# Plain second token product, an earlier hash and a plainly stored last row in an attention and mixer kernel

## The chip, the cores and the metric

The kernel runs on one core of a Trainium2 chip. The metric is the device time of one execution in microseconds (us); lower is better. Time before: 816.98 us, the median of three runs (815.75 to 818.22). The profiled execution spans 815.1 us from its first instruction to its last.

## The reference

Hash attention, then one mixer block. There are 4 batches, 8 heads, 768 tokens and 64 values per head; all is float32.

```python
def _attn_ref(q, k, v, proj):
    q_bits = (np.einsum('bhsd,dk->bhsk', q, proj) > 0)      # 6 bits, likewise k_bits
    ...                                                     # bucket = sum of bits * powers of two
    mask = q_bucket[:, :, :, None] == k_bucket[:, :, None, :]
    scores = scale * np.matmul(q, k.transpose(0, 1, 3, 2))
    scores = np.where(mask, scores, -1000000000.0)
    ...                                                     # softmax over the keys
    return np.matmul(attn, v)

def _moe_ref(x, w_tok1, w_tok2, w_ch1, w_ch2):              # x: (4, 768, 512)
    xt = x.transpose(0, 2, 1)
    h = np.maximum(xt @ w_tok1, 0.0) @ w_tok2               # token mixing: 768 -> 256 -> 768
    u = x + h.transpose(0, 2, 1)
    h2 = np.maximum(u @ w_ch1, 0.0) @ w_ch2                 # channel mixing: 512 -> 1536 -> 512
    return u + h2
```

## The kernel before

It has three stages: attention over 16 pairs of heads (a batch `b` and two heads `hp` each), the token products of the four batches, and the channel products. `XT` holds x and then u for the whole problem in on-chip memory, with channels on the partitions. Each engine takes its instructions in order, and waits where their inputs or buffers aren't ready.

**Attention.** Every pair has two halves of 384 queries. The hash bits of the next pair are made by a matmul, a comparison on VectorE, a scaling on ScalarE, and eight small DMAs that spread the rows. The first pair's bits are made in another way (`first_hashes`).

```python
        def hashes(n):
            g = pool.tile([P, HALF], BF16, name="g", tag="g", bufs=2)
            ps = psum.tile([P, 2, 512], F32, name="hp", tag="sc", bufs=3)[:, 0]
            for j in range(4):
                ...                                          # matmul hp <- projection, qk
            nc.vector.tensor_scalar(g, ps[:, :HALF], 0.0, 0.5, op0=ALU.is_gt, op1=ALU.subtract)
            nc.scalar.mul(g, g, bitscale)
            for j in range(4):
                for i in range(2):
                    ...
                    nc.sync.dma_start(out=bitrows[n % 2][...], in_=g[at : at + NB + 1])

        for n in range(len(pairs)):
            ...
            for now in halves:
                now.scores()        # sc <- qk, sc <- bits on TensorE, e <- sc on ScalarE
                now.add()           # sums of e on VectorE
                if now.half == 0:
                    now.add_last()
            if before:
                before.sums()
            if n + 1 < len(pairs):
                hashes(n + 1)
            halves[1].add_last()
            ...
            halves[0].weigh()       # acc <- e, v on TensorE
```

**Token stage.** `mix1` makes the first product (6 matmuls of 512 columns for each of two blocks) with its relu. `mix2` is the second product and the residual: plain for batch 0, and for batches 1 to 3 by Strassen's scheme in Winograd's form, with seven products of a half-sized matmul in place of eight, sums of the left blocks (`left_sums`) and of the weights (`weight_sums`) on VectorE. The result is assembled in one of three staging places, and a DMA that adds puts it into `XT`. Between these, `job()` takes one piece from a list: the sums of the first channel weights, then the conversion of w_ch2 from doubles (`slot`).

```python
        def mix2(b, m):
            ...
            ps = [bank("t2")[:, :HALF] for _ in range(4)]        # 8 PSUM banks in turn
            to = places[(2 * b + m + 1) % 3]...
            p1, u, p7, p57 = ...                                 # four quarters of that place

            def store():
                nc.gpsimd.dma_start(
                    out=XT[:, m::2, S * b : S * b + S], in_=to..., accum_op=ALU.add,
                )

            if not b:
                ...                                              # 8 plain matmuls, 4 copies on ScalarE
                return store()
            product(0, a00, b00)
            nc.scalar.copy(p1, ps[0])                            # line 695
            product(1, a01, b10)
            product(2, s1, sums[:, 0])
            nc.scalar.copy(p57, ps[2])                           # line 698
            product(3, new[:, 1], b01)
            nc.scalar.copy(p7, ps[3])                            # line 700
            product(0, new[:, 0], sums[:, 1], False)
            nc.scalar.copy(u, ps[0])                             # line 702
            product(2, new[:, 2], b11, False)
            product(3, a11, sums[:, 2], False)
            nc.vector.tensor_tensor(p1, ps[1], p1, op=ALU.add)   # line 705
            nc.gpsimd.tensor_tensor(p57, p7, p57, op=ALU.add)    # line 706
            nc.vector.tensor_tensor(p57, p57, u, op=ALU.add)     # line 707
            nc.vector.tensor_tensor(p7, ps[3], u, op=ALU.add)    # line 708
            nc.vector.tensor_tensor(u, ps[2], u, op=ALU.add)     # line 709
            store()                                              # line 673

        for b in range(B):
            mix1(b)
            if b:
                left_sums(b)
                mix2(b - 1, 0)
                job()
                mix2(b - 1, 1)
            if b == 1:
                weight_sums()
        mix2(B - 1, 0)
        inputs(0, T, 0)                                          # sums for the channel stage
        mix2(B - 1, 1)
```

**Channel stage.** All is Strassen there, in two groups of token columns. Line 774 is the matmul of a helper that the whole stage uses, 780 a copy out of PSUM. A group's outputs come from seven products, p1 to p7. Most output blocks are stored by a GpSimd DMA that adds to a residual (u) stored there earlier by a plain DMA. In the last product of the last group (p4, with `final`), VectorE completes four quarters, and each goes out by a plain DMA of its own.

```python
            if final:                                             # end of product(), p4 of the last group
                nc.vector.tensor_tensor(qs[:, 3], qs[:, 3], u, op=ALU.add)
                ...
                for i, a in [(1, ps[2]), (2, ps[3])]:
                    nc.vector.tensor_tensor(qs[:, i], a, qs[:, i], op=ALU.add)          # line 1193
                    (nc.scalar if i == 2 else nc.sync).dma_start(out=final(...), in_=qs[:, i])
                return
            ...
                product(s, 5, "p2", q2, [*end, add(q7, q7, XT[:, KC:, sl[0]])])
                product(s, 6, "p4", q7, [
                    add(q2, q2, q1), store(q2, 0, 0),             # adding store of the first row, 512 KB
                ], lambda i, n: out[...])
```

Of the kernel before, what the change touches and what calls it, by code (L numbers as in the profile page):

```python
# [48 lines left out]
def kernel(  # L49
# [14 lines left out]
    P = 128  # L64
# [75 lines left out]
    class Conversion:  # L140


        def __init__(self, pool, parts, bufs, apart=False):
            self.pool, self.bufs, self.apart = pool, bufs, apart
            self.todo = [
                (w, dst, rows, j, n)
                for w, dst, rows, blocks in parts
                for j in range(*blocks, rows)
                for n in range(0, dst.shape[2], NW // rows)
            ]  # L150
            self.fetched, self.begun, self.ready = [], None, None
            for _ in range(bufs - 1):
                self.fetch()
# [17 lines left out]
        def begin(self):  # L171
            if not self.fetched:
                return
            raw, to, rows = self.fetched.pop(0)
            hi = raw[:, :, 1]
            tmp = self.pool.tile([P, 2, NW], F32, name="tmp", tag="cvt", bufs=1)
            big = tmp[:, 0].bitcast(U32)

            nc.vector.tensor_scalar(  # L179
                big, hi, 3, 0x3FFFFFFF, op0=ALU.logical_shift_left, op1=ALU.bitwise_and,  # L180
            )
            nc.vector.scalar_tensor_tensor(
                big, hi, 0xC0000000, big, op0=ALU.bitwise_and, op1=ALU.bitwise_or,
            )
            self.begun = raw, tmp, to, rows
# [16 lines left out]
        def end(self):  # L202
# [5 lines left out]
            hi = size  # L208
            if self.apart:
                size = self.pool.tile([P, NW], F32, name="size", tag="size", bufs=1)  # L210
            nc.scalar.activation(size, hi, ACT.Square)
# [11 lines left out]
        def slot(self):  # L223

            self.end()
            self.fetch()
            self.begin()
            self.join()

# [6 lines left out]
    def bounce(stage, n):  # L236

        b, hp = pairs[n]
        stage = stage.rearrange("p (a k i) -> p a k i", k=2, i=32)
# [26 lines left out]
    def attention(pool, psum, W1, W2, x0):  # L266
# [202 lines left out]
        for n in range(len(pairs)):  # L469
# [3 lines left out]
            for now in halves:  # L473
                now.scores()
                now.add()
                if now.half == 0:
                    now.add_last()
            if before:
                before.sums()
            if n + 1 < len(pairs):  # L480
                hashes(n + 1)
# [21 lines left out]
            if n and n % 2 == 0:  # L503
                bounce(pool.tile([P, 2 * S], F32, name="stage", tag="stage", bufs=1), n - 2)
# [93 lines left out]
    def tokens(pool, psum, W1, W2, x0, weights, jobs, T, places):  # L598

# [7 lines left out]
        if not turned:  # L607
            fetch(1, x1)
            jobs = jobs(weights(pool))
            bounce(places[2], len(pairs) - 2)  # L610
        NQ = DM // 2
        sums = pool.tile([P, 3, HALF], F32, name="W2sums", tag="W2sums", bufs=1)
        b00, b01, b10, b11 = (W2[:, k, HALF * n : HALF * n + HALF] for k in range(2) for n in range(2))

        def weight_sums():
            nc.vector.tensor_tensor(sums[:, 0], b01, b00, op=ALU.subtract)
            nc.vector.tensor_tensor(sums[:, 1], b11, sums[:, 0], op=ALU.subtract)
            nc.vector.tensor_tensor(b01, b11, b01, op=ALU.subtract)
            nc.vector.tensor_tensor(sums[:, 2], b10, sums[:, 1], op=ALU.subtract)
# [11 lines left out]
        def mix1(b):  # L631
# [16 lines left out]
            if b % 2:  # L648
                new = pool.tile([P, 3, NQ], F32, name="r1s", tag="r1s", bufs=1)
            else:  # L650
                new = T[0].rearrange("p k t -> p (k t)")[:, : 3 * NQ].rearrange("p (i c) -> p i c", i=3)
            R1[b] = r1, new
# [3 lines left out]
        def left_sums(b):  # L656
            r1, new = R1[b]
            a00, a01, a10, a11 = (r1[:, k, NQ * i : NQ * i + NQ] for i in range(2) for k in range(2))
            nc.vector.tensor_tensor(new[:, 1], a00, a10, op=ALU.subtract)
            nc.vector.tensor_tensor(a10, a10, a11, op=ALU.add)  # L660
            nc.vector.tensor_tensor(new[:, 0], a10, a00, op=ALU.subtract)
            nc.vector.tensor_tensor(new[:, 2], a01, new[:, 0], op=ALU.subtract)

        def mix2(b, m):

            r1, new = R1[b]
            a00, a01, s1, a11 = (r1[:, k, NQ * i : NQ * i + NQ] for i in range(2) for k in range(2))
            ps = [bank("t2")[:, :HALF] for _ in range(4)]
            to = places[(2 * b + m + 1) % 3].rearrange("p (i n t) -> p i n t", i=2, n=2)
            p1, u, p7, p57 = (to[:, i, n] for i in range(2) for n in range(2))  # L670

            def store():
                nc.gpsimd.dma_start(  # L673
                    out=XT[:, m::2, S * b : S * b + S], in_=to.rearrange("p i n t -> p i (n t)"),
                    accum_op=ALU.add,
                )

            if not b:
                for n in range(4):
                    for k in range(NJ):  # L680
                        at = P * m + NQ * (n // 2)
                        nc.tensor.matmul(  # L682
                            ps[n], r1[:, k, at : at + P], W2[:, k, HALF * (n % 2) : HALF * (n % 2) + HALF],
                            start=(k == 0), stop=(k == NJ - 1),
                        )
                    nc.scalar.copy(to[:, n // 2, n % 2], ps[n])  # L686
                return store()

            def product(at, left, right, start=True):
                nc.tensor.matmul(  # L690
                    ps[at], left[:, P * m : P * m + P], right, start=start, stop=True, skip_group_check=True,
                )

            product(0, a00, b00)
            nc.scalar.copy(p1, ps[0])
            product(1, a01, b10)
            product(2, s1, sums[:, 0])
            nc.scalar.copy(p57, ps[2])
            product(3, new[:, 1], b01)
            nc.scalar.copy(p7, ps[3])  # L700
            product(0, new[:, 0], sums[:, 1], False)
            nc.scalar.copy(u, ps[0])
            product(2, new[:, 2], b11, False)
            product(3, a11, sums[:, 2], False)
            nc.vector.tensor_tensor(p1, ps[1], p1, op=ALU.add)  # L705
            nc.gpsimd.tensor_tensor(p57, p7, p57, op=ALU.add)  # L706
            nc.vector.tensor_tensor(p57, p57, u, op=ALU.add)
            nc.vector.tensor_tensor(p7, ps[3], u, op=ALU.add)
            nc.vector.tensor_tensor(u, ps[2], u, op=ALU.add)
            store()  # L710

        for b in range(B):
            mix1(b)
            if b:
                left_sums(b)
                mix2(b - 1, 0)
                job()
                mix2(b - 1, 1)
            if b == 1:
                weight_sums()  # L720
        mix2(B - 1, 0)
        inputs(0, T, 0)
        mix2(B - 1, 1)
# [22 lines left out]
    def channels(pool, psum, SW1, second, TA, judge):  # L746
# [278 lines left out]
        def prepare():  # L1025
# [42 lines left out]
            def hidden_parts(name):  # L1068
# [9 lines left out]
                [], sums, [whole("p1"), second_parts("p7")], *([second_parts(name)] for name in ("p6", "p3", "p5", "p2", "p4")),  # L1078
# [67 lines left out]
        def product(s, j, name, q, between, final=None):  # L1146
# [38 lines left out]
            nc.vector.tensor_tensor(p57[:, 0], p57[:, 0], p57[:, 1], op=ALU.add)  # L1185
            if final:
# [16 lines left out]
        def outputs(s):  # L1203
# [46 lines left out]
            else:  # L1250
                product(s, 5, "p2", q2, [*end, add(q7, q7, XT[:, KC:, sl[0]])])
                product(s, 6, "p4", q7, [
                    add(q2, q2, q1), store(q2, 0, 0),
                ], lambda i, n: out[KC + i, :, sl[0].start + TT // 2 * n : sl[0].start + TT // 2 * (n + 1)])

        def residual(s):

            for i in range(2):
                for n in range(2):
                    if s < last or (i, n) != (1, 0):  # L1260
# [98 lines left out]
    def attention_and_tokens(W1, W2, x0):  # L1359
# [13 lines left out]
        def weights(pool):  # L1373
            return Conversion(pool, [(w_ch2, WC2, 3, (0, NHT))], bufs=3, apart=True)

        def jobs(conversion):
            early, late = weight_sums(
                WC1, SW1, slice(0, NCB // 2), slice(NCB // 2, NCB), slice(0, DCH // 2), slice(DCH // 2, DCH),
            )
            return [  # L1380
                lambda: (early(), late()),
                *[conversion.slot] * (NHT * DM // NW + 1),
            ]

        SW2 = second["SW2"].rearrange("p i k c -> p i (k c)")
        places = [SW2[:, i] for i in range(3)]
        inside(tokens, W1, W2, x0, weights, jobs, [TA[:, 0], None, TA[:, 1], None], places)

    def careful_attention_and_tokens(W1, W2, x0):
        def weights(pool, psum):  # L1390
            conversion = Conversion(pool, [(w_tok1, W1, 3, (0, NR)), (w_tok2, W2, 1, (0, NJ))], bufs=3)
            while conversion.fetched or conversion.ready:
                conversion.slot()
# [8 lines left out]
        with tc.tile_pool(name="places", bufs=1, reuse_waits="tile") as pool:  # L1402
            places = [pool.tile([P, 2 * S], F32, name=f"place{i}") for i in range(3)]
            inside(tokens, W1, W2, x0, None, None, [TA[:, 0], None, TA[:, 1], None], places)
# [50 lines left out]
```

## Time and profile before

| engine | busy us | share of the span | what it does |
|---|---|---|---|
| TensorE (PE) | 799.5 | 98% | 3889 matmul records; two for one float32 matmul |
| weight load (PEld) | 473.8 | 58% | beside the matmuls |
| VectorE (DVE) | 667.7 | 82% | sums, conversion, assembly of products |
| ScalarE (ACT) | 441.5 | 54% | exponentials, copies out of PSUM |
| GpSimd (POOL) | 60.1 | 7% | a few sums, adding DMAs |

The profile shows one execution. By TensorE's timeline the attention lasts until 317.5 us, the token stage from there to 405.65 us, and the channel stage from there on; the last matmul ends at 808.2 us. A row of the timeline is start, length, engine, line, operation, output and inputs, shapes, count, and in brackets the idle time before it with what ended it. Busy shares are averages over stages; what a change in one stage is worth has to be read from TensorE's idle time in that stage. The names are the program's: in the token stage the staging places lie in the tile named `second`, the PSUM banks are `t`, `tmp` and `raw` belong to the conversion.

### The profile page before, as it was taken

What the parts mean: (1) busy time and instruction counts of PE and PEld (TensorE: products, weight loads), DVE (VectorE), ACT (ScalarE), POOL (GpSimd) and SP (SyncE); (2) the same over time, 40 slices, a digit from 0 to 9 for tenths busy, and PEclk for the clock granted to TensorE, in tenths of its full rate; (3) what the DMA queues carried; (4) which work ended last, traced back from release to release, by engine and by line L of the source; (5) the groups of instructions that cost most, each with busy time, mean ns of one, the idle gap of its engine ahead of it and who ended that gap; (6) DMA issues with size and microseconds to landing.
All of it is one profiled execution on the core that took longest, in us unless ns stands there. A gap on an engine that the chain in (4) does not pass through costs nothing.

```text
span 815.1 us, 10615 instructions
## 1 busy us (share of the span) xinstructions
PE 799.5 (98%) x3889; PEld 473.8 (58%) x3889; DVE 667.7 (82%) x877; ACT 441.5 (54%) x707; POOL 60.1 (7%) x83
## 2 busy tenths in 40 slices
PE   9999999999999999999699999999999999999996
PEld 5544444444444444454344448876666886676885
DVE  4789999999998677989468678897669897778985
ACT  5688888888888885333122221236774335775111
POOL 1000000000000000012311110011010012000001
PEclk9999999999999999999899999999999999999999
DMA  4435353537353415885745785499754578740455
GB/s 159 152 124 157 119 158 120 158 119 237 147 166 99 138 42 174 262 212 127 183 75 200 265 330 188 173 276 263 258 138 146 203 229 206 231 118 1 155 179 113
DMA packets 90669, 138.62 MB, mean 170 GB/s; under 512 B 29608, under 2 KB 62832, under 8 KB 88304
## 3 DMA queue, kind: packets, MB, share of 16 engines
q1 hardware_dynamic: 82320, 112.60, 41.4%
q0 software_dynamic: 7728, 24.64, 13.6%
q8 instruction: 33, 0.54, 0.3%
q10 hardware_dynamic: 560, 0.61, 0.2%
q14 instruction: 28, 0.23, 0.1%
HBM read 97.21 MB, written 33.69 MB: 161 GB/s over the span
## 4 chain that ended last, share of the span: by engine, by line
PE 92%; DVE 3%; issue 2%; POOL 1%; SPq 1%; ACT 0%; DMA 0%; DVEq 0%; POOLq 0%; ACTq 0%
PE b L774 49%; PE sc L345 18%; PE acc L397 15%; PE t L639 4%; PE sums L421 2%; PE t L682 1%; PE t L690 1%; PE hp L306 1%; DVE esd L383 1%; PE hw L324 1%; SPq L316 1%; POOL second L706 0%; PE idle L459 0%; POOL XT L673 0%; DVE tmp L179 0%
## 5 line engine op out<-in xcount | busy, mean ns | idle before, releaser
L352 ACT ACTIVATE e<-sc 128x768 f32<-128x768 f32 x192 | 154.2, 810 | 15.7 <-PE sc L345 15.4
L345 PE MATMUL sc<-qk 64*128 64x384 f32 x768 | 157.1, 488 | 0.0
L774 PE MATMUL b<-R,second 128*128 128x256 f32 (+1 forms) x612 | 150.9, 404 | 0.0
L774 PEld LDWEIGHTS b<-R,second 128*128 128x128 f32 x612 | 116.3, 190 | 31.6 <-issue 17.2
L780 ACT COPY c<-b 128x512 f32<-128x512 f32 (+1 forms) x78 | 37.4, 488 | 174.8 <-PE b L774 170.7
L397 PE MATMUL acc<-e,vn 128*64 128x384 f32 x768 | 127.6, 488 | 0.0
L383 DVE TENSOR_TENSOR esd<-esd,e 128x768 f32<-128x768 f32 x96 | 92.0, 958 | 10.0
L345 PEld LDWEIGHTS sc<-qk 64*128 64x128 f32 x768 | 68.1, 187 | 48.4 <-issue 46.0
L397 PEld LDWEIGHTS acc<-e,vn 128*64 128x64 f32 x768 | 53.6, 137 | 73.2 <-issue 71.8
L774 PE MATMUL b<-XT,WC 128*128 128x256 f32 (+1 forms) x264 | 84.3, 464 | 2.5 <-DVE second L705 2.5
L774 PEld LDWEIGHTS b<-XT,WC 128*128 128x128 f32 x264 | 50.7, 192 | 34.0 <-issue 26.0
L345 PE MATMUL sc<-bits 64*128 64x384 bf16 x384 | 64.1, 323 | 0.8 <-DMA bits<-g 0.6
L379 DVE SCALAR_TENSOR_TENSOR esd<-e 128x768 f32<-128x768 f32 x32 | 30.3, 948 | 19.5 <-ACT e L352 19.4
L639 PE MATMUL t<-x,W 128*128 128x512 f32 x96 | 41.8, 593 | 0.0
L673 POOL DMA_DIRECT2D XT<-second x8 | 9.9, 1237 | 385.3 <-ACT second L686 340.2
L442 ACT COPY rec<-rec 32x384 f32<-32x384 f32 x64 | 32.6, 509 | 10.0 <-DVE rec L436 9.5
L345 PEld LDWEIGHTS <-bits 64*128 64x128 bf16 x384 | 20.2, 94 | 26.8 <-DMA bits<-g 1.4
L774 PE MATMUL b<-XT,SW 128*128 128x256 f32 (+1 forms) x120 | 34.6, 422 | 0.0
L774 PE MATMUL b<-TA,WC 128*128 128x512 f32 x72 | 33.8, 592 | 0.0
L774 PE MATMUL b<-TA,SW 128*128 128x512 f32 x72 | 32.9, 592 | 0.0
L386 DVE TENSOR_TENSOR esd<-esd,e 128x768 f32<-128x768 f32 x32 | 30.5, 953 | 1.8
L639 PEld LDWEIGHTS t<-x,W 128*128 128x128 f32 x96 | 18.2, 190 | 22.7 <-issue 21.5
(212 smaller groups left out, 1151.5 us busy)
## 6 DMA issues: line engine op xcount, KB each, us to landing
second<-left SPq DMA_DIRECT2D x18, 1344.0 KB
raw<-in_moe_w_ch SPq DMA_DIRECT2D x16, 768.0 KB
qk<-in_qk SPq DMA_DIRECT2D x15, 768.0 KB
seen<-in_qk POOLq DMA_DIRECT2D x21, 384.0 KB, 3.8
WC<-hidden_left SPq DMA_DIRECT2D x15, 448.0 KB
vn<-in_v SPq DMA_DIRECT2D x16, 384.0 KB
vt<-in_vT SPq DMA_DIRECT2D x16, 384.0 KB
x<-bounced SPq DMA_DIRECT2D x4, 1536.0 KB
```

Source lines behind the costliest of these rows:

```text
L345: nc.tensor.matmul(sc[:, i, :HALF], t[rows, 1, P * c : P * c + P], t[rows, 0, qs], start=start, stop=not start,)
L352: nc.scalar.activation(e, sc[:, :, :HALF], ACT.Exp, scale=SCALE)
L379: nc.vector.scalar_tensor_tensor(self.d, es[0], NR * EPS, es[1], op0=ALU.add, op1=ALU.add,)
L383: nc.vector.tensor_tensor(self.d, self.d, e, op=ALU.add)
L386: nc.vector.tensor_tensor(self.d, self.d, self.es[-1], op=ALU.add)
L397: nc.tensor.matmul(acc[D * i : D * i + D], vn[:, i, c], e[:, i], start=(c == 0), stop=(c == NR - 1),)
L421: nc.tensor.matmul(ps[at : at + 32], ones[:, :32], self.halves[h].d[:, i], start=True, stop=True,)
L442: nc.scalar.copy(rec[other : other + 32, h], rec[at : at + 32, h])
L639: nc.tensor.matmul(ps, W1[:, r, P * j : P * j + P], x[:, r], start=(r == 0), stop=(r == NR - 1),)
L673: nc.gpsimd.dma_start(out=XT[:, m::2, S * b : S * b + S], in_=to.rearrange("p i n t -> p i (n t)"), accum_op=ALU.add,)
L774: nc.tensor.matmul(ps, left(k), right(k), start=start and k == ks[0], stop=stop and k == ks[-1], skip_group_check=True,)
L780: nc.scalar.copy(c, ps)
```

## The change

Three things are changed together.

1. The second token product is plain in all four batches. Each of its eight PSUM banks of a batch is added straight into `XT` by VectorE. The staging places, copies, left and weight sums, GpSimd's sum and the adding DMAs fall away. With the place freed, the conversion keeps two temporary tiles, and its piece (`one`) finishes the block before the current one last of all. Two jobs come in each plain product.
2. The hash bits of the second pair are made between the two halves of the first pair.
3. In the last group, the first output row too is completed on VectorE, residual included, in the second-last product (p2), and goes out by plain DMAs; the residual for it is no longer stored beforehand.

```diff
-            for _ in range(bufs - 1):
+            for _ in range(bufs - 1 or 1):
...
-            tmp = self.pool.tile([P, 2, NW], F32, name="tmp", tag="cvt", bufs=1)
+            tmp = self.pool.tile([P, 2, NW], F32, name="tmp", tag="cvt", bufs=self.bufs - 1)
...
-        def slot(self):
-            self.end()
-            self.fetch()
+        def one(self):
+            before, self.ready = self.ready, None
             self.begin()
             self.join()
+            self.ready, after = before, self.ready
+            self.end()
+            self.ready = after
+            self.fetch()
...
                 now.scores()
+                if n == now.half == 0:
+                    hashes(1)
                 now.add()
...
-            if n + 1 < len(pairs):
+            if 0 < n < len(pairs) - 1:
                 hashes(n + 1)
...
-        def left_sums(b):
...
-        def mix2(b, m):
...
-            store()
+        def mix2(b):
+            r1 = R1.pop(b)
+            for cb in range(NCB):
+                for half in range(2):
+                    ps = bank("t2")
+                    for j in range(NJ):
                         nc.tensor.matmul(
+                            ps[:, :HALF], r1[:, j, P * cb : P * cb + P],
+                            W2[:, j, HALF * half : HALF * half + HALF],
+                            start=(j == 0), stop=(j == NJ - 1),
                         )
+                    u = XT[:, cb, S * b + HALF * half : S * b + HALF * half + HALF]
+                    nc.vector.tensor_tensor(u, ps[:, :HALF], u, op=ALU.add)
+                if cb % 2:
+                    job()
 
         for b in range(B):
             mix1(b)
             if b:
-                left_sums(b)
-                mix2(b - 1, 0)
-                job()
-                mix2(b - 1, 1)
-            if b == 1:
-                weight_sums()
-        mix2(B - 1, 0)
-        inputs(0, T, 0)
-        mix2(B - 1, 1)
+                mix2(b - 1)
+            if b == 2:
+                inputs(0, T, 0)
+        mix2(B - 1)
...
             return [
-                [], sums, [whole("p1"), second_parts("p7")], ...
+                sums, [whole("p1"), second_parts("p7")], ...
...
             nc.vector.tensor_tensor(p57[:, 0], p57[:, 0], p57[:, 1], op=ALU.add)
+            if j < 6 and final:
+                begin(ORDER[j + 1])
             if final:
...
-                product(s, 5, "p2", q2, [*end, add(q7, q7, XT[:, KC:, sl[0]])])
-                product(s, 6, "p4", q7, [
-                    add(q2, q2, q1), store(q2, 0, 0),
-                ], lambda i, n: out[...])
+                product(s, 5, "p2", q1, [*end, add(q1, q1, XT[:, :KC, sl[0]])], final(0))
+                product(s, 6, "p4", q7, [add(q7, q7, XT[:, KC:, sl[0]])], final(KC))
...
-                    if s < last or (i, n) != (1, 0):
+                    if s < last or n:
                         ...                                     # residual stored by plain DMA
```

## The prediction

> **What bounds the kernel now.** I read the page's busy shares and chain first, then TensorE's own waits, then the timeline of the three places that the change touches: the start, the token stage, the end.
>
> ```profile
> PE 799.5 (98%) x3889; PEld 473.8 (58%) x3889; DVE 667.7 (82%) x877; ACT 441.5 (54%) x707; POOL 60.1 (7%) x83
> PE 92%; DVE 3%; issue 2%; POOL 1%; SPq 1%; ACT 0%; DMA 0%; DVEq 0%; POOLq 0%; ACTq 0%
> ```
>
> TensorE is busy 98% of the span and is 92% of the chain. So a part of the change pays only if it takes matmuls away, or closes one of the few holes in TensorE's row. All waits that TensorE's row has are these (engine, line, waited for, us in total, times, longest):
>
> ```profile
> PE t L690 <- ACT second L695: 4.4, 1, 4.4
> PE b L774 <- DVE second L705: 2.5, 1, 2.5
> PE idle L459 <- DVE ones L97: 1.0, 1, 1.0
> PE sc L345 <- DMA bits<-g: 0.6, 2, 0.3
> ```
>
> The two large ones lie in the token stage. Its TensorE timeline (start, length, line, operands, count, and in brackets the idle time before), cut to the start and the end of the stage:
>
> ```profile
> 317.54 20.87 PE L639 MATMUL t<-x,W 128*128 128x512 f32 x48
> 338.24 10.48 PE L682 MATMUL t<-W,r 128*128 128x384 f32 x32
> 348.56 10.46 PE L639 MATMUL t<-x,W 128*128 128x512 f32 x24
> ...
> 394.07 0.81 PE L690 MATMUL t<-W,r1s 128*128 128x384 f32 x2
> 399.26 1.48 PE L690 MATMUL t<-W2sums,r1s 128*128 128x384 f32 x2 [4.38 <-ACT second L695]
> 400.53 1.48 PE L690 MATMUL t<-W,r1s 128*128 128x384 f32 x2
> 401.81 1.34 PE L690 MATMUL t<-W2sums,r 128*128 128x384 f32 x2
> 405.65 5.40 PE L774 MATMUL b<-XT,WC 128*128 128x512 f32 x8 [2.49 <-DVE second L705]
> 410.88 1.45 PE L774 MATMUL b<-TA,WC 128*128 128x512 f32 x3
> ```
>
> Each f32 matmul is two records. The start times give the price of a record: (338.24 - 317.54)/48 = 0.431 us at 512 columns, (348.56 - 338.24)/32 = 0.3225 us at 384. The reader is to see that after each hole the clock is halved as well: from 399.26 on, two records take 1.28 us instead of 0.645, and the first eight of the channel stage take 410.88 - 405.65 = 5.23 us instead of 8 x 0.431 = 3.45.
>
> Why the 4.38 us hole? The rows of GpSimd, ScalarE and VectorE at that time:
>
> ```profile
> 389.75 1.21 POOL L673 DMA_DIRECT2D XT<-second  x1 [6.99 <-DVE second L709]
> 398.73 0.48 ACT L695 COPY second<-t 128x384 f32<-128x384 f32 x1 [7.20 <-DMA XT<-second]
> 388.78 0.56 DVE L709 TENSOR_TENSOR second<-t,second 128x384 f32<-128x384 f32 x1
> 401.24 0.56 DVE L707 TENSOR_TENSOR second<-second 128x384 f32<-128x384 f32 x1 [7.13 <-POOL second L706]
> ```
>
> The results of the product go through a ring of three staging places and an adding DMA into XT. The last copy (L695) needs the place whose DMA was issued at 389.75, because VectorE had finished that result only at 389.3, some 4 us behind TensorE; it lands about 9 us later, at 398.7. So the hole is not work: it is staging, DMA latency and VectorE's lag. The 2.49 us hole is the same lag again: L707 waits for GpSimd, L705 behind it frees the PSUM bank that the next stage wants.
>
> **What the Trainium skill says.** "TensorE: Matmul & The Clock Gate", Part 1 (What's actually happening): the array falls to half clock after an idle window of about 3.4 us and needs about as long a busy one to come back. This trace agrees: 4.38 us idle, then records at twice their time for about 4 us, and again after the 2.49 us. "DMA: Bandwidth & Descriptors", SWDGE vs HWDGE vs iDMA: a DMA that adds must be issued by GpSimd; plain ones go out from SyncE or ScalarE. Here the eleven adding stores to the output took 6.1 us at least to land, and the adding ones to XT 6.3 to 8.9. "GPSIMD Engine Reference", 1. Specifications: GpSimd shares its SBUF interface with VectorE, which contends in a two-port mode or with two SBUF inputs. Fitting, though not proof: the L179 of 371.06 took 2.12 us instead of 0.56 beside GpSimd's L673 and L706.
>
> **Part 1, token product without Strassen in batches 1 to 3.** It costs matmuls. A plain batch has 16 (32 records), a Strassen batch 14 (28 records). Three batches: 3 x 4 x 0.3225 = **+3.9 us**. In return the copies, GpSimd's add, the places and the adding DMA go: VectorE adds each PSUM bank straight into XT.
> Does TensorE now run without holes? Work of the stage: 96 x 0.431 + 128 x 0.3225 = 41.4 + 41.3 = 82.7 us, so it would end at 317.5 + 82.7 = 400.2, if VectorE keeps up. I played its queue through with durations of before: one conversion 5.2 us (335.70 to 340.94), a PSUM add 0.47 in a row (368.08 to 368.55), free for conversions at 329.5. Two conversions to 340.9 (the second waits for ScalarE's square behind the relu at 339.0); four adds of batch 0 as their banks come, to 344.1; conversion to 349.3; four adds to 351.2; three conversions to 366.9; adds of batch 1. TensorE needs the first of their banks back at 369.2, for batch 3's first product: VectorE gives it at 367.4, **1.8 us of margin**, the tightest point. After that: second four adds at 375.8, conversion 381, inputs 383.4, last conversion piece 384.4, and batch 2's banks, wanted again from 389.9, have 5 us. VectorE is done with the last bank some 0.5 us after TensorE, and the channel stage starts on banks freed earlier. So no hole: the stage ends at 400.2 instead of 405.65, **-5.4**, and the channel stage starts at full clock, 5.23 - 3.45 = **-1.8**. Together -7.2 (the +3.9 is inside).
> The channel stage's weight sums come one job slot sooner. TensorE shows no wait there for them now and its next use of those banks is two hidden blocks away: 0.
>
> **Part 2, the second pair's hash bits earlier.** Now g (L310) comes behind nine of VectorE's sums, and eight small DMAs follow one by one, so pair 1's scores begin before their bits are there. VectorE, SyncE and TensorE:
>
> ```profile
> 23.77 0.55 DVE L310 TENSOR_SCALAR g<-hp 128x384 bf16<-128x384 f32 x1
> 25.07 6.09 SPq L316 DMA_DIRECT2D bits<-g  x8
> 29.36 0.33 PE L345 MATMUL sc<-bits 64*128 64x384 bf16 x1 [0.32 <-DMA bits<-g]
> ```
>
> With a second one at 32.28 the waits listed are 0.6 us, but pair 1's scores take 39.01 - 27.74 = 11.27 us and pair 2's 58.22 - 48.32 = 9.90: the hole is worth **1.3 us** (a wait's length leaves out what the queue loses around it). Made between the halves, the hash product runs at 14.0, g is ready at about 15.5, and the eight DMAs are through by about 24, ahead of 27.7. TensorE does the same 0.8 us of work at 14.0 instead of 19.07. ScalarE's scaling (0.6 us) slips between the exponentials; TensorE runs three PSUM tiles ahead of it. Gain -1.3, and I see no cost: qk of the second pair was issued at 1.7, and the transfers of the start are over by 12.
>
> **Part 3, the last group's first row.** The end now:
>
> ```profile
> 804.31 1.20 POOL L1213 DMA_DIRECT2D out<-second  x1 [6.61 <-DVE c L1181]
> 808.25 0.76 DVE L1193 TENSOR_TENSOR second<-b,second 128x256 f32<-128x256 f32 x2
> 809.04 0.37 ACTq L1194 DMA_DIRECT2D out<-second  x1
> ```
>
> Matmuls end at 808.2, the last store is issued at 809.04, the span ends at 815.1. The 512 KB adding store of 804.31 still moves data until about 810 (the software queue has half of the DMA engines' time from 809 to 810), so the four last stores of 128 KB stand behind it and trickle until 812.6. Afterwards p2 is complete on VectorE and goes out plainly around 798 to 803, with nothing large beside the last stores: I estimate that they land **1 us** sooner.
> VectorE pays in p2: one add of 0.34 for p1, and 0.45 + 4 x 0.35 in place of 0.34 + 0.60 for the other quarters, about 1.7 us later in all. Then p4's b00 (L1165, now at 800.50) is ready at about 803.4; TensorE wants it at 804.16. And the add of 1.22 us that p4 loses (p2 + p1) is replaced by the one of the residual for row two. VectorE reaches L1182 at about 806.0 as now, where it idles 1.86 us today. So no loss, with 0.7 us to spare.
>
> **Sum.** -7.2 - 1.3 - 1.0 = -9.5: 816.98 becomes 807.5. I add 0.5 for small collisions in the two places with thin margins: **808.0 us**, 1.1% faster.
>
> **Rivals.** (a) VectorE becomes the bound of the token stage. It would do 32 PSUM adds (15 us) and eight conversions (42 us), with sums and inputs some 70 us of the 83. For it: the lead of 1.8 us at batch 3 is small, and a conversion now fetches its next raw block only after its last operation, so the sixth block has 5.2 us to land before it is wanted. Against it: GpSimd's disturbance goes, and some 5 MB of adding DMA with it. If it holds, TensorE stands for 2 to 4 us and may lose its clock for a further 2: 811 to 813. (b) The holes were only postponed: TensorE's saved wait comes back in the channel stage, as VectorE begins it with the WC2 sums (7 us) in the middle of the first block. Against: four bank pairs, and no wait of TensorE's there now. It would leave just parts 2 and 3 and the matmuls' price, +3.9 - 2.3: 818 to 819. (c) The end doesn't move, because the fixed time after the last landing rules and not the collision: 809. (d) The price of the matmuls is paid and the restart at half clock is not spared, because another short wait takes its place: 811.
>
> **Range and chances.** (a) in a mild form, (c) and (d) lie within 804.5 to 812; (b) I give one in twelve. The other way, 804.5 would need the disturbance of VectorE to have cost elsewhere too. Faster by over 2% would be under 800.6, more than all holes together: 0.03. Within 2%: 0.96. Slower by over 2%: 0.01.
>
> **What would show it.** Token matmuls without a gap, batches 1 to 3 with 32 records each, channel stage 82.7 us after the token stage's start and its first eight records in 3.45 us; pair 1's scores in 9.9 us and no wait for bits; no adding DMA after the one of p3, last packets about 1 us closer to the last matmul. A wait of TensorE (L-line of the token or channel product) for VectorE's add into XT, or of VectorE for raw, would prove (a) and put the time above 810; a wait for R or c in the first channel blocks would prove (b).

## The result, and the profile after

The changed kernel takes **807.34 us** (median; 806.26 to 808.27), the kernel before 817.6 us when run beside it. The ratio is 0.9873, with a 95% interval of 0.9856 to 0.9891. The profiled execution spans 805.7 us in place of 815.1.

The page's busy shares and its chain of the changed kernel:

```profile
PE 797.0 (99%) x3901; PEld 473.5 (59%) x3901; DVE 665.6 (83%) x874; ACT 427.2 (53%) x675; POOL 41.2 (5%) x68
PE 97%; DMA 1%; DVE 1%; issue 0%; ACTq 0%; DVEq 0%
```

TensorE has 12 records more (3901 against 3889) and is all the same busy for 2.5 us less. That isn't a contradiction: by stage its busy time changes by -1.4 us at the start, -0.8 in pair 1's scores, +1.4 in the token stage and -1.8 in the first eight channel records. In the last two places records at half clock are gone; what happened at the start is told with the sum below. The chain is 97% TensorE, from 92%.

TensorE's waits in the changed kernel, all of them (engine, line, waited for, us in total, times, longest):

```profile
PE idle L459 <- DVE ones L97: 1.0, 1, 1.0
PE hw L324 <- DMA qk<-in_qk: 0.9, 1, 0.9
PE sc L345 <- DVE bits L328: 0.2, 1, 0.2
```

Both holes of the token stage and the wait for bits from a DMA are gone; what is left lies in the first 11 us. Of it only the 0.9 us for qk is new: the 0.2 us for bits from VectorE was there before too, though the prediction's list leaves it out. TensorE's timeline of the token stage (start, length, line, operands, count; the idle time would stand in brackets):

```profile
315.70 20.87 PE L631 MATMUL t<-x,W 128*128 128x512 f32 x48
336.41 10.48 PE L650 MATMUL t<-W,r 128*128 128x384 f32 x32
...
377.65 20.80 PE L650 MATMUL t<-W,r 128*128 128x384 f32 x64
398.29 3.60 PE L717 MATMUL b<-XT,WC 128*128 128x512 f32 x8
401.72 1.88 PE L717 MATMUL b<-TA,WC 128*128 128x512 f32 x4
```

There is no bracket in it: the stage runs from 315.70 to 398.29 = 82.59 us, and the first eight records of the channel stage take 401.72 - 398.29 = 3.43 us. VectorE at the place with the thinnest margin, and at the stage's end:

```profile
363.12 0.95 DVE L209 SCALAR_TENSOR_TENSOR second<-raw,tmp 128x768 f32<-128x768 f32 x1
363.99 1.94 DVE L656 TENSOR_TENSOR XT<-t,XT 128x384 f32<-128x384 f32 x4
...
397.19 0.56 DVE L656 TENSOR_TENSOR XT<-t,XT 128x384 f32<-128x384 f32 x1 [0.73 <-PE t L650]
398.49 0.56 DVE L656 TENSOR_TENSOR XT<-t,XT 128x384 f32<-128x384 f32 x1 [0.73 <-PE t L650]
```

Batch 1's adds begin at 363.99. The PSUM banks are used in a ring of eight, so the bank that TensorE wants at 367.35, for batch 3's first product, is the one that the first of these adds frees, at about 364.5 (an add takes 0.55 us). From the fourth bank of batch 2 to the last of batch 3 VectorE waits 0.73 us for every bank: there it is TensorE that sets the pace.

The start and the end of pair 1's scores on TensorE, and the last matmuls with the last store:

```profile
27.28 0.92 PE L345 MATMUL sc<-qk 64*128 64x384 f32 x4
37.17 0.85 PE L421 MATMUL sums<-esd,ones 128*32 128x384 f32 x8
...
795.00 4.05 PE L717 MATMUL b<-R,second 128*128 128x256 f32 x18
799.96 0.34 ACTq L1139 DMA_DIRECT2D out<-second  x1
```

Laid beside each other by TensorE's start times, and with the last matmul's end at 808.21 and 799.05:

| stretch | before, us | after, us | difference | predicted |
|---|---|---|---|---|
| start to pair 1's scores | 27.74 | 27.28 | -0.46 | 0 |
| pair 1's scores | 11.27 | 9.89 | -1.38 | -1.3 |
| token stage | 88.11 | 82.59 | -5.52 | -5.4 |
| first eight channel records | 5.23 | 3.43 | -1.80 | -1.8 |
| rest of the channel stage | 397.33 | 397.33 | 0.00 | 0 |
| last matmul's end to the span's end | 6.89 | 6.65 | -0.24 | -1.0 |

The lines sum to -9.4 us, the whole difference of the two spans: the attention after pair 1's scores takes 278.53 us in both (39.01 to 317.54, and 37.17 to 315.70). The medians differ by 10.3 us, while the executions of the kernel before lie between 815.75 and 819.71; the table is that of the two profiled executions alone.

### The profile page after: what moved, and what is told of

The parts are those of the page before. It is cut to its first block, busy times and chain, and to the rows that moved or that the text cites. A ratio compares the mean times of both kernels' runs of the same rounds, so it can differ in the third digit from the quotient of the medians.

```text
span 805.7 us, 10554 instructions
## 1 busy us (share of the span) xinstructions
PE 797.0 (99%) x3901; PEld 473.5 (59%) x3901; DVE 665.6 (83%) x874; ACT 427.2 (53%) x675; POOL 41.2 (5%) x68
## 4 chain that ended last, share of the span: by engine, by line
PE 97%; DMA 1%; DVE 1%; issue 0%; ACTq 0%; DVEq 0%
PE b L717 49%; PE sc L345 19%; PE acc L397 16%; PE t L631 5%; PE t L650 5%; PE sums L421 2%; PE hp L306 1%; DMA qk<-in_qk 1%; PE hw L324 0%; DVE second L1152 0%; DVE R L1111 0%; DVE R L1108 0%; DVE q L1138 0%; DVE second L1138 0%; DVE bits L326 0%
## 5 line engine op out<-in xcount | busy, mean ns | idle before, releaser
L717 PE MATMUL b<-XT,WC 128*128 128x256 f32 (+1 forms) x264 | 82.5, 456 | 0.0
L650 PE MATMUL t<-W,r 128*128 128x384 f32 x128 | 41.8, 486 | 0.0
L650 PEld LDWEIGHTS t<-W,r 128*128 128x128 f32 x128 | 24.3, 190 | 17.6 <-issue 1.4
```

Of the source, the lines that this page charges most:

```text
L650: nc.tensor.matmul(ps[:, :HALF], r1[:, j, P * cb : P * cb + P], W2[:, j, HALF * half : HALF * half + HALF], start=(j == 0), stop=(j == NJ ...
L717: nc.tensor.matmul(ps, left(k), right(k), start=start and k == ks[0], stop=stop and k == ks[-1], skip_group_check=True,)
```

## Experiments

### The hash bits back in their old place

```diff
-                if n == now.half == 0:
-                    hashes(1)
...
-            if 0 < n < len(pairs) - 1:
+            if n + 1 < len(pairs):
                 hashes(n + 1)
```

> The changed kernel with the second pair's hash bits back behind the first pair's second half; all else as changed. Theory (the hash part is worth the hole in pair 1's scores and nothing else): pair 1's scores take 11.2 to 11.4 us again instead of 9.9, TensorE waits for bits again, the token stage stays at 82.6 us, and the time is 1.3 to 1.5 us above the changed kernel, about 808.7. Rival (the attention's earlier end was mostly the luck of the start, where the first hash matmuls ran at another clock): 0 to 0.5 us above.

It took 808.9 us, 1.6 above the changed kernel's 807.34. Its trace has the old wait back, and pair 1's scores take 37.93 - 26.66 = 11.27 us; the token stage stays at 82.58. The view of TensorE's waits, cut to that line:

```profile
PE sc L345 <- DMA bits<-g: 0.6, 2, 0.3
```

So 0.6 us in the list of waits stands for 1.4 us of time. The start of pair 1's scores was even earlier here (26.66), without the early hash: the 0.46 us of the table's first line are scatter of the start, not the hash's work. The rival holds for those 0.46 us only.

### The first row stored by the adding DMA

The end of the last group as before (p2 into q2, its sum with q1 and the adding store in p4, the residual stored ahead), all else as changed.

```diff
-                product(s, 5, "p2", q1, [*end, add(q1, q1, XT[:, :KC, sl[0]])], final(0))
-                product(s, 6, "p4", q7, [add(q7, q7, XT[:, KC:, sl[0]])], final(KC))
+                product(s, 5, "p2", q2, [*end, add(q7, q7, XT[:, KC:, sl[0]])])
+                product(s, 6, "p4", q7, [add(q2, q2, q1), store(q2, 0, 0)], ...)
```

> The changed kernel with the last group's first row again stored by the adding DMA. Theory from the trace (the end after the last matmul is 6.65 us against 6.89, because a thin trail of packets and a fixed time follow the bulk): 0.2 to 0.3 us above the changed kernel, not to be told from zero by the times, but seen in the trace as 6.9 us after the last matmul. Rival (my prediction: the adding store holds up the four last ones): 1.0 us above.

It took 808.55 us (807.68 to 811.48), 1.2 above the changed kernel; its trace ends 6.92 us after the last matmul. As the two disagree, it was run again beside the changed kernel itself, on one chip:

> The changed kernel itself, beside the two that follow, on one chip. Expected: 807.0 to 808.0 us, token stage 82.6 us, 6.65 us from the last matmul's end to the end of the span.

> The changed kernel with the last group's first row stored by the adding DMA, once more, as the first runs stood 1.2 us above the changed kernel's while the trace shows only 0.27 us at the end. Theory (the trace is right, the rest was the chip's or the start's scatter): 0.2 to 0.5 us above the changed kernel of this call, 6.9 us after the last matmul. Rival (the row is worth the 1 us of the prediction, and the profiled execution was a lucky one): 0.9 us or more above, and over 7.2 us after the last matmul.

The changed kernel took 807.06 us (806.31 to 807.96), the other 808.05 (807.81 to 808.48): 1.0 apart, with ratios to before of 0.9872 (0.9855 to 0.989) and 0.9889 (0.9872 to 0.9905), whose intervals overlap. In the traces the ends are 6.84 and 6.84 us, but the changed kernel's trace is that of its slowest execution (807.96) and the other's that of its second fastest (807.95), so these two traces can't show where the 1.0 us lies. Taken over all traces of this study in which the full set of last stores goes out, the end takes 6.40 to 6.91 us with the row stored plainly (eight kernels, mean 6.73) and 6.84 to 6.99 with the adding store (four, mean 6.91). So the traces show 0.2 us, with ranges that overlap, the times about 1 us, and the two are not reconciled: neither theory is settled. How far medians of one and the same TensorE timeline scatter is seen in the kernel with two idle sums (below): 807.76 us on another chip, 0.7 above the 807.06 here.

### Strassen kept, the other two parts changed

```diff
                 now.scores()
+                if n == now.half == 0:
+                    hashes(1)
                 now.add()
...
+                product(s, 5, "p2", q1, [*end, add(q1, q1, XT[:, :KC, sl[0]])], final(0))
+                product(s, 6, "p4", q7, [add(q7, q7, XT[:, KC:, sl[0]])], final(KC))
```

> The kernel before with parts 2 and 3 alone: Strassen, staging places and adding DMAs stay in the token stage. Theory (the token part carries 7.3 us of the change, and the three parts simply add up): token stage 88 us, first eight channel records 5.2 us, time 7.3 us above the changed kernel, 814.5 to 815. Rival (the token holes move with the start of the stage or with its DMA traffic): the holes differ by over 2 us from 4.4 and 2.5, and the time lies outside 813 to 816.

It took 815.17 us (ratio to before 0.9979, 0.9968 to 0.9989), 7.8 above the changed kernel. The token stage takes 404.32 - 316.33 = 87.99 us, the first eight channel records 5.24, and the holes are the same:

```profile
PE t L692 <- ACT second L697: 4.2, 1, 4.2
PE b L776 <- DVE second L707: 2.5, 1, 2.5
```

The stage began 1.2 us earlier than before, and the holes didn't move. In the trace the token product accounts for 87.99 + 5.24 - 82.59 - 3.43 = 7.2 us.

### Strassen, places and adding DMAs, but little conversion

Five of the six VectorE operations of each w_ch2 block in the token stage are left out, so the channel weights are not the real ones; the amount of matmul work is the same.

```diff
         def begin(self):
             ...
+            if self.light:
+                self.begun = raw, tmp, to, rows
+                return
...
+            if self.light:
+                self.ready = hi, hi, to, rows
+                return
```

> The kernel before, with five of the six VectorE operations of each w_ch2 conversion of the token stage left out (so the channel weights are not the real ones); Strassen, places and adding DMAs stay. Theory (VectorE's lag behind TensorE made the holes): VectorE keeps up, token stage 79 to 80 us, no wait of TensorE over 1 us in it, first eight channel records at 3.45 us, time 10 to 11 us below before, about 807. Rival (the adding DMAs, which follow one another and take 6 to 9 us each against TensorE's 4.5 us per half product, make them): a hole of 3 us or more stays at the end of the stage or moves into the first channel blocks, and the time stays above 811.

It took 809.18 us, 7.8 below before. The token stage takes 400.97 - 320.19 = 80.78 us and the first eight records 3.54. The rows of TensorE, GpSimd, VectorE and ScalarE in which something is left:

```profile
397.90 0.91 PE L697 MATMUL t<-W2sums,r1s 128*128 128x384 f32 x2 [0.77 <-ACT second L702]
400.97 3.70 PE L781 MATMUL b<-XT,WC 128*128 128x512 f32 x8 [0.87 <-DVE second L715]
408.83 1.96 PE L781 MATMUL b<-TB,SW 128*128 128x512 f32 x4 [0.73 <-DVE TB L602]
...
388.33 1.21 POOL L680 DMA_DIRECT2D XT<-second  x1 [3.15 <-DVE second L716]
397.60 1.22 POOL L680 DMA_DIRECT2D XT<-second  x1 [7.04 <-issue]
...
399.89 0.56 DVE L714 TENSOR_TENSOR second<-second 128x384 f32<-128x384 f32 x1 [7.20 <-POOL second L713]
...
397.37 0.48 ACT L702 COPY second<-t 128x384 f32<-128x384 f32 x1 [3.59 <-DMA XT<-second]
```

VectorE has idle time ahead of batch 2 and finishes the batch's first half 2.6 us behind TensorE (387.92 against 385.36), where it was 6.3 behind before (389.34 against 383.02). The holes shrink from 6.9 us to 2.4 (the last 0.73 of it in the channel stage), without a stretch at half clock behind them. So its lag made most of them, as the prediction said. But not all. The DMA of 388.33 lands after 9.0 us, and the copy of 397.37 waits for it: that is the hole of 0.77. The second adding DMA of batch 2 has its result at 392.2 and goes only at 397.60, just after that landing; GpSimd's sum stands in the queue behind it, and VectorE behind that sum: this lies behind the other two holes. The profile names nothing that the DMA of 397.60 waited for; that it waited for the landing, 0.3 us earlier, is concluded from the times. Two other issues for which its timeline names nothing, of 378.16 here and of 398.96 in the kernel before, come 0.3 us after a landing too. The latter stands at the same place, with its result ready at 393.6 and the DMA of 389.75 ahead of it landed at about 398.7:

```profile
398.96 1.22 POOL L673 DMA_DIRECT2D XT<-second  x1 [6.97 <-issue]
```

The rival is right about this remainder. With 2.4 us it is about what the time lies above my theory.

### How much room VectorE has

```diff
         def mix2(b):
             r1 = R1.pop(b)
+            if b == 1 and not turned:
+                for _ in range(2):                # 6 in the second kernel
+                    nc.vector.tensor_tensor(x0[:, 0:3, :DTOK], W1[:, 0:3], W1[:, 3:6], op=ALU.add)
```

> The changed kernel with two idle sums of 128x768 (0.96 us each) on VectorE ahead of batch 1's adds. Theory (in the changed kernel's trace the add that frees the bank for batch 3's first product ends at about 364.9, and TensorE wants the bank at 367.35, so 2.4 us of margin): TensorE runs through, token stage 82.6 us, time as changed within 0.3 us. Rival (VectorE is already the bound of the stage): 1.5 to 2 us above.

> The same with six idle sums (5.7 us). Theory: a hole of 5.7 - 2.4 = 3.3 us ahead of batch 3's first product, perhaps followed by matmuls at half clock for some us, so 3.3 to 5.5 us above the changed kernel; nothing more after it, as VectorE has slack in batches 2 and 3. Rival (the margin lies elsewhere or is much larger): no hole, within 0.5 us. Rival (all of VectorE's time counts): 5.7 us or more above.

With two sums: 807.76 us, token stage 397.86 - 315.27 = 82.59 us, no new wait. With six: 812.2 us, and one hole, in the place foreseen. VectorE's and TensorE's rows of the second kernel:

```profile
363.76 5.91 DVE L648 TENSOR_TENSOR x<-W 128x768 f32<-128x768 f32 x6
369.59 1.94 DVE L659 TENSOR_TENSOR XT<-t,XT 128x384 f32<-128x384 f32 x4
...
370.20 12.26 PE L631 MATMUL t<-x,W 128*128 128x512 f32 x24 [2.92 <-DVE XT L659]
382.30 20.80 PE L653 MATMUL t<-W,r 128*128 128x384 f32 x64
```

The 24 records take 382.30 - 370.20 = 12.10 us in place of 10.30: a hole of 2.9 us has 1.8 us of half clock behind it. The stage takes 402.94 - 315.47 = 87.47 us, 4.9 more. Batch 3's first product would have begun at 356.79 + 10.32 = 367.11 and began 3.1 us later: of the 5.8 us given to VectorE 2.7 were free, the rest counted one for one, and the clock came on top. TensorE goes on at 370.20, when the first of the four adds is done (369.59 + 0.55). In the changed kernel's trace that add ends 2.8 us before TensorE wants the bank, which agrees with 2.7; the 2.4 expected had counted to the end of the second add. This is what rival (a) of the prediction would have looked like.

### One last store in place of four

The stores of three quarters of the last output row are left out, so that part of the output is not written; the one issued last stays.

```diff
-            if final:
+            if final and j < 6:
                 nc.sync.dma_start(out=final(0, 0), in_=qs[:, 0])
...
+                    if j < 6 or i == 2:
                         (nc.scalar if i == 2 else nc.sync).dma_start(out=final(i // 2, i % 2), in_=qs[:, i])
```

> The changed kernel with three of the four last stores (128 KB each) left out, so three quarters of the last output row are not written; the store issued last stays. Theory (the end is the latency of the last store and what follows it): the span ends 6.4 to 6.65 us after the last matmul, time as changed within 0.3 us. Rival (the four stores stand behind one another): 1 us or more less.

It took 806.67 us, 1.1 below the kernel with two idle sums of the same chip, whose TensorE timeline is the changed one's; its end takes 804.6 - 798.77 = 5.83 us, 0.8 less than in the changed kernel. The store that is left goes out 0.91 us after the last matmul's end in both. My theory of a pure latency falls: with the other three stores out of the way it is through about 0.8 us sooner (0.6 to 1.1 against the eight traces above). That is as large as what I had put down to the adding store ahead of them.

### Strassen for the last batch alone, straight from PSUM

```diff
+            product(0, a00, b00)
+            product(1, a01, b10)
+            product(2, new[:, 3], sums[:, 0])
+            product(3, new[:, 1], sums[:, 3])
+            add(0, 0, 0)                         # XT quarter (0,0) += PSUM bank 0, on VectorE
+            product(0, new[:, 0], sums[:, 1], False)
+            add(1, 1, 2)
+            add(0, 0, 1)
...                                               # seven products, nine adds in all per half
-        mix2(B - 1)
+            seven(B - 1, 0)
+            seven(B - 1, 1)
```

> The changed kernel with Strassen's seven products again for the last batch alone, but its parts added straight from PSUM into XT by VectorE (18 adds in place of 8, plus 8 sums of left blocks and weights), without places, copies or adding DMAs. Theory (VectorE idles 0.73 us of each 1.29 us in batches 2 and 3, so this work is free there): TensorE loses four records of 0.3225 us, token stage 81.3 us, time 1.3 us below the changed kernel, about 806.0. Rival (VectorE falls behind at the end of the stage and the channel stage waits for its input sums or banks): a wait of TensorE of 1 us or more in the first channel block, time at or above the changed kernel's.

> The changed kernel with the last batch's second product by Strassen with sums straight from PSUM, once more beside the changed kernel on the same chip. Expected: 1.3 us below it (four records of 0.3225 us), token stage 81.3 us; what the first run showed beyond that would be the start's scatter.

It took 805.7 us and, beside the changed kernel, 806.6 against 807.06. The token stage takes 395.96 - 314.67 = 81.29 us in the first run and 396.32 - 315.03 = 81.29 in the second, 1.30 less than in the changed kernel, and TensorE waits for nothing new. The end of the stage on VectorE and TensorE in the first run:

```profile
389.07 7.86 DVE L691 TENSOR_TENSOR XT<-t,XT 128x384 f32<-128x384 f32 x16 [0.73 <-PE t L686]
397.98 0.56 DVE L691 TENSOR_TENSOR XT<-t,XT 128x384 f32<-128x384 f32 x1
...
395.32 0.81 PE L686 MATMUL t<-x,r 128*128 128x384 f32 x2
395.96 3.60 PE L773 MATMUL b<-XT,WC 128*128 128x512 f32 x8
```

VectorE ends 2.6 us after TensorE, and nothing waits for it: the channel stage begins on banks of the first half. Against before the ratios are 0.987 (0.9852 to 0.9889) and 0.9873 (0.9855 to 0.9892). The traces show the 1.3 us; the times lie on both sides of it (2.1 us below the kernel with two idle sums of the same chip, 0.5 below the changed kernel beside it) and don't resolve it. In the kernel before the holes lay in this very batch and at its end. Here its seven products run without one, with no staging places and no adding DMAs, and with a VectorE that isn't behind when they begin.

## Why the prediction was right

- **The bound.** Right. TensorE's order decides: in parts 1 and 2, where its work and its holes were counted, the trace followed within 0.2 us.
- **Part 1.** Right in both terms: -5.5 and -1.8 us measured for -5.4 and -1.8. The plain product costs its 12 records and removes two holes and two stretches at half clock that were dearer. VectorE kept up, with a margin of 2.8 us by the trace and 2.7 by the six idle sums where I had 1.8; a conversion takes 5.03 us (354.04 to 359.07) rather than 5.2. The cause of the holes was right in the main but not complete: with little conversion work on VectorE 2.4 us of 6.9 remain, behind adding DMAs that land late and go one after another. The 2.49 us hole, which I called the same lag again, hangs on this too: GpSimd's sum stands behind the DMA of 398.96.
- **GpSimd's disturbance of VectorE.** No run takes it by itself. After the change no conversion operation of the stage takes longer than 0.96 us, where one took 2.12 before; that fits, and is no proof.
- **Part 2.** Right: 1.38 us for 1.3, and undone by putting the hash back. What the list of waits names was less than half of it.
- **Part 3.** The failed term is "I estimate that they land **1 us** sooner". In the traces the end is shorter by 0.2 us. The bulk did come sooner: of the data bytes moved from 3 us before the last matmul's end on, nine tenths were through 2.6 us after it before, and 2.2 in the changed kernel. But the last packets of the four stores came 4.4 us after it in both (at 812.6 and 803.4), and the end of the span followed these, 2.5 and 2.3 us later. The reason given, the adding store ahead of the last four, was not the main delay: three of the four removed brought 0.8 us. Whether the row is worth more than 0.2 us in executions that weren't profiled stays open, as the times put it at 1 us twice. The other half of the step held: p4's b00 was ready at 794.2, and TensorE took it at 795.00, 0.8 us later, for the 0.7 of the prediction.
- **The rivals.** (a) didn't come, but the idle sums show that it was less than 3 us away. (b) didn't come: the rest of the channel stage is 397.33 us in both kernels, though the WC2 sums now begin at 408.21 (421.93 before), within its first block. (c) came about for the trace. (d) didn't come.
- **The sum.** In the profiled execution the 0.8 us missing from part 3 were made up by 0.46 us of the start, which is scatter, and 0.2 us more from parts 1 and 2, and the sum came out at 9.4 for 9.5. Pair 1's scores began between 26.25 and 27.90 us in all traces but one, whatever the kernel (30.39 in the one with little conversion). The first four hash records alone took 2.93 us before and 1.62 in the changed kernel, which then waited 0.9 us for qk. So the sum is met by luck in part. The stated 808.0 held 0.5 us more for collisions that didn't come, which goes against the 0.8 us missing from part 3; this too is luck.
- **Slips in the working that changed nothing.** VectorE finished batch 2's first half 6.3 us behind TensorE, not some 4. The terms given for its extra work in p2 add up to 1.25 us, not 1.7; the trace has 1.73 (from p2's first add to p4's b00 3.46 us before, 5.19 in the changed kernel). The adding DMAs to XT took up to 10.5 us to land, not 8.9.

## What to carry to other kernels

A saving of matmuls has to be weighed with what it hangs on: here 3.9 us of matmuls saved brought 6.9 us of waits and some 3.7 us of half clock (1.9 behind the first hole, 1.8 behind the second), because VectorE's queue ran behind, with conversions and the scheme's sums in it, and the adding DMAs went one after another, so that buffers came free late. Where TensorE is the bound, play the queue of the engine that frees its buffers through, piece by piece, and look for the smallest margin; a few idle operations of known length in that place show whether it is what you think. And take such a scheme up again where the other engine idles, as in the last batch (1.3 us in the trace), rather than everywhere.

## What the hardware showed that was not expected

- **A hole of 1.9 to 2.9 us was enough to halve the clock.** "TensorE: Matmul & The Clock Gate", Part 1 (What's actually happening), puts the idle window at about 3.4 us; the prediction counted the hole of 2.49 us as agreeing with that, and it doesn't. The clock had come back in between (granted 1.00 from 403 to 405 us) and fell again (0.50 from 407 to 409), which cost 1.8 us; the kernel with Strassen kept did the same with 2.54 us. A single hole of 2.92 us, in the kernel with six idle sums, also cost 1.8 us more behind it. And in the run with little conversion a hole of 1.88 us at the start was followed by half clock (granted 0.50 from 13 to 15 us; the rows stand below). Holes of 0.77 and 0.87 us in the same run left the next eight records at 3.54 us for 3.43. Where between 0.9 and 1.9 us it begins, and on what else it depends, no run here shows.

```profile
10.54 0.91 PE L331 MATMUL hw<-qk,projs 128*128 128x384 f32 x2 [1.88 <-DMA qk<-in_qk]
12.75 1.49 PE L352 MATMUL sc<-qk 64*128 64x384 f32 x4
17.58 0.81 PE L352 MATMUL sc<-qk 64*128 64x384 f32 x4
```

- **DMAs that add are slow for their size.** "DMA: Bandwidth & Descriptors", Anatomy of one DMA, fits 2.0 us + bytes/436e3 for a DMA issued by GpSimd; for the 768 KB into XT that makes an estimate of 3.8 us. The eight of the kernel before landed after 6.3 to 10.5 us. The one of 398.96, ready 5.3 us earlier, went only when the one ahead of it had landed; all of them go into one tile.
